# Lightweight convolution and SiLU feed-forward in float32: silu(h) as the stationary operand of the second product, chunks in groups of eight by product shape

## The chip, the cores and the metric

One core of a Trainium2 chip. The number to be predicted is the device time of one execution in microseconds (us), as a median over runs. Engines are written as in the profile: PE is TensorE's matmul, PEld its weight load, DVE is VectorE, ACT is ScalarE, POOL is GpSimd and SP is SyncE, which here issues most of the DMAs.

## The reference

The input x is 8 sequences of 4096 tokens with 192 channels. A causal convolution of 7 taps per head (8 heads of 24 channels, softmax over a head's taps) is followed by a feed-forward block with 2048 hidden units:

```
w = softmax(weight, axis=-1)                      # (8 heads, 7 taps)
x1[b, s, c] = sum_k w[head(c), k] * x_pad[b, s + k, c]
h = x1.reshape(32768, 192) @ w_in                 # w_in (192, 2048)
g = h * (1 / (1 + exp(-h)))                       # silu
out = g @ w_out                                   # w_out (2048, 192)
```

The two matrices arrive as float64 and are rounded to float32 on the chip. All products run in float32.

## The kernel before

The 32768 tokens are worked off in 64 blocks of 512. `load` (L70 to L73) brings a block's rows into `nat`, tokens on partitions. `turn_in` (L180 to L192) turns it on the PE with eight 128x128 transposes into two PSUM tiles `pt`, which ACT copies to `xt`. `conv` (L194 to L204) applies the taps on the DVE, 14 instructions, and leaves `cv`: the first half holds channels 0 to 127 ("a"), the second the other 64 channels ("b") twice, once in each half of the partitions.

The 2048 hidden units are 16 chunks of 128, taken as 8 pairs q. `up` (L207 to L217) makes h of a pair: two products with 128 rows of weights (L210, shape 128\*128 in the profile), then two with 64 rows (L212, 64\*128), which stand in different rows of the PE and run side by side; then ACT writes g = silu(h). `down` (L219 to L237) adds the pair into the block's sums, channels on partitions: the weights w_out are stationary and g moves, 512 columns at a time, into 128 channels (L226, 128\*128) and into 64 (L230, 128\*64), the latter for the two chunks side by side in different columns of the PE. After the eighth pair the sums go to `ot` (L235 on ACT, L236 on DVE). `turn_out` (L239 to L249) turns them back on the PE, four transposes (L246) and four products with `ident2` (L247) that also add the two side-by-side sums, and the DVE copies them to `osb`, which goes out by DMA.

The loop (L254 to L273) sets the order by hand: `up` of pair q, then `down` of pair q - 1. In block b, `turn_in` of block b + 1 comes with q = 1, its `conv` with q = 1 and 2, and `turn_out` of block b - 1 with q = 2. In block 0, `round_w(q)` (L112 to L143, 12 DVE instructions per pair) rounds the weights of a pair ahead of its `up`. A framework places instructions on each engine and adds the waits; each engine runs its own in order.

In the profile a float32 product is two passes, each with a weight load of its own: the 1024 products of L210 show as 2048 MATMULs and 2048 LDWEIGHTS. "Pass" below is one such MATMUL. A transpose is one pass.

Of the kernel before, what the change touches and what calls it, by code (L numbers as in the profile page):

```python
# [9 lines left out]
F32 = mybir.dt.float32  # L10
I32 = mybir.dt.int32
AF = mybir.ActivationFunctionType
ALU = mybir.AluOpType
# [4 lines left out]
def kernel(  # L18
# [5 lines left out]
    moe_w_out: bass.AP,  # L24
    out: bass.AP,
):
    """Everything runs in float32, with channels on partitions between the two turns.

    The two matrices come as float64, which the engines don't have: as raw bits, rounded to
    float32 here (to nearest even; below float32's normal range to 0).  # L30
    A block is TB tokens. Its rows are turned on the PE, the taps are applied along the free axis
    on the DVE, and h = w_in.T @ xT, g = silu(h), oT = w_out.T @ g follow; oT is turned back.
    The D = 192 channels are P = 128 ("a") and R = 64 ("b"). The b rows are held twice, in
    both halves of the partitions, so that the K = 64 products of two chunks of h run side by
    side in the rows of the PE; the M = 64 products of two chunks of g run side by side in its
    columns, and the product that turns their two sums back also adds them.
    """
    nc = tc.nc
    PSUM = bass.MemoryType.PSUM

    B, S, D = x.shape
    H, K = weight.shape
    NT = B * S
    DFF = moe_w_in.shape[1]
    P = 128
    R = D - P
    grp = D // H
# [3 lines left out]
    NB = NT // TB  # L51
    NCH = DFF // P
    NQ = NCH // 2
    assert R == 64 and D == H * grp and S % TB == 0 and DFF == 2 * P * NQ and NQ >= 3

    x_v = x.flatten_outer_dims().rearrange("(n s p) d -> n p s d", s=SUBS, p=P)
# [2 lines left out]
    const = ctx.enter_context(tc.tile_pool(name="const", bufs=1))  # L59
    wpool = ctx.enter_context(tc.tile_pool(name="wp", bufs=3))  # L60
    xpool = ctx.enter_context(tc.tile_pool(name="xp", bufs=3))
    gpool = ctx.enter_context(tc.tile_pool(name="gp", bufs=3))
    opool = ctx.enter_context(tc.tile_pool(name="op", bufs=2))
    ps_h = ctx.enter_context(tc.tile_pool(name="ps_h", bufs=2, space=PSUM))
    ps_o = ctx.enter_context(tc.tile_pool(name="ps_o", bufs=1, space=PSUM))
    ps_t = ctx.enter_context(tc.tile_pool(name="ps_t", bufs=2, space=PSUM))

    nats, xts, cvs, gs, accs, ots = ({} for _ in range(6))

    def load(b):  # L70
        nat = nats[b] = xpool.tile([P, SUBS, P + 2 * R], F32, tag="nat", name="nat")
# [2 lines left out]

    load(0)

    # Each partition's logits: channel c has those of head c // grp.
    wraw = const.tile([P, 2, K], F32, name="wraw")
    for half, p0, c0, c1 in ((0, 0, 0, P), (1, 0, P, D), (1, R, P, D)):
        c = c0  # L80
# [7 lines left out]
            )  # L88
            c = e

    # For a pair of chunks: 2P columns of w_in's a rows, P of its b rows (the first chunk's on
    # partitions 0 to R, the second's above), and D of w_out for each chunk.
    WA, WB, WO = 2 * P, 3 * P, 3 * P + 2 * D
    in32 = moe_w_in.bitcast(I32)
    out32 = moe_w_out.bitcast(I32).rearrange("(q e p) d -> q p e d", e=2, p=P)
# [16 lines left out]
    def round_w(q):  # L112
        words = raws.pop(q).rearrange("p (n t) -> p n t", t=2)
        lo, hi = words[:, :, 0], words[:, :, 1]
        sc, ex, mh, ml, st = (
            wpool.tile([P, WO], I32, tag=f"w_{n}", name=f"w_{n}", bufs=1)
            for n in ("sc", "ex", "mh", "ml", "st")
        )
        m = wpool.tile([P, WO], F32, tag="w_m", name="w_m", bufs=1)

        def two(out, in_, s1, op0, s2, op1):
            nc.vector.tensor_scalar(out, in_, scalar1=s1, scalar2=s2, op0=op0, op1=op1)  # L122

        # sc: the sign and the exponent, as the bits of a float32.
        two(ex, hi, 20, ALU.logical_shift_right, 0x7FF, ALU.bitwise_and)
        two(ex, ex, 896, ALU.max, 896 + 255, ALU.min)
        two(ex, ex, 896, ALU.subtract, float(1 << 23), ALU.mult)
        two(sc, hi, 31, ALU.logical_shift_right, 31, ALU.logical_shift_left)
        nc.vector.tensor_tensor(sc, sc, ex, op=ALU.bitwise_or)
        # The mantissa's upper 21 bits, its next 23, and whether any of the last 9 is set: the  # L130
        # sum of the three rounds once, as the whole would.
        two(mh, hi, 0xFFFFF, ALU.bitwise_and, 0x100000, ALU.bitwise_or)
        nc.vector.tensor_single_scalar(ml, lo, 9, op=ALU.logical_shift_right)
        nc.vector.tensor_single_scalar(st, lo, 0x1FF, op=ALU.bitwise_and)
        nc.vector.tensor_single_scalar(st, st, 1, op=ALU.min)
        nc.vector.scalar_tensor_tensor(  # L136
            out=m, in0=ml, scalar=2.0, in1=st, op0=ALU.mult, op1=ALU.add
        )
        nc.vector.scalar_tensor_tensor(
            out=m, in0=mh, scalar=float(1 << 24), in1=m, op0=ALU.mult, op1=ALU.add  # L140
        )
        nc.vector.scalar_tensor_tensor(  # L142
            out=ws[q], in0=m, scalar=2.0**-44, in1=sc.bitcast(F32), op0=ALU.mult, op1=ALU.mult  # L143
        )

    def w_in_a(q, e):
        return ws[q][:, ts(e, P)]

    def w_in_b(q, e):
        return ws[q][R * e : R * e + R, WA:WB]  # L150

    def w_out_a(q, e):
        return ws[q][:, WB + D * e : WB + D * e + P]

    def w_out_b(q, e):
        return ws[q][:, WB + D * e + P : WB + D * e + D]

    for q in range(NQ):
        load_w(q)
# [1 line left out]

    ident = const.tile([P, P], F32, name="ident")
    make_identity(nc, ident)
    # ident2[p, r] is 1 where p % R == r.
    ident2 = const.tile([P, R], F32, name="ident2")
    nc.vector.tensor_tensor(ident2, ident[:, 0:R], ident[:, R:P], op=ALU.add)

    wmax = const.tile([P, 2], F32, name="wmax")
    wexp = const.tile([P, 2, K], F32, name="wexp")
    wsum = const.tile([P, 2], F32, name="wsum")  # L170
# [9 lines left out]
    def turn_in(b):  # L180
# [5 lines left out]
            nc.gpsimd.tensor_copy(xt[:, :, 0:pad], xts[b - 1][:, :, TB : TB + pad])  # L186
        xts.pop(b - 1, None)
        for half in range(2):
            pt = ps_t.tile([P, TB], F32, tag="pt", name="pt")
            for s in range(SUBS):  # L190
                nc.tensor.transpose(pt[:, ts(s, P)], nat[:, s, ts(half, P)], ident)  # L191
            nc.scalar.copy(xt[:, half, pad : pad + TB], pt)  # L192
# [11 lines left out]
                    out=dst, in0=src[:, k : k + TB], scalar=tap, in1=dst, op0=ALU.mult, op1=ALU.add  # L204
                )

    def up(b, q):  # L207
        hs = [ps_h.tile([P, TB], F32, tag=f"h{e}", name=f"h{e}") for e in range(2)]
        for e in range(2):
            nc.tensor.matmul(hs[e], w_in_a(q, e), cvs[b][:, 0, :], start=True, stop=False)  # L210
        for e in range(2):
            nc.tensor.matmul(  # L212
                hs[e], w_in_b(q, e), cvs[b][R * e : R * e + R, 1, :], start=False, stop=True
            )
        gs[b, q] = [gpool.tile([P, TB], F32, tag=f"g{e}", name=f"g{e}") for e in range(2)]
        for e in range(2):
            nc.scalar.activation(gs[b, q][e], hs[e], AF.Silu)  # L217

    def down(b, q):  # L219
        if q == 0:  # L220
            accs[b] = [ps_o.tile([P, TB], F32, tag=f"acc{i}", name=f"acc{i}") for i in range(2)]
        g = gs.pop((b, q))
        acc_a, acc_b = accs[b]
        first, last = q == 0, q == NQ - 1
        for e in range(2):
            nc.tensor.matmul(  # L226
                acc_a, w_out_a(q, e), g[e], start=first and e == 0, stop=last and e == 1
            )
        for e in range(2):
            nc.tensor.matmul(  # L230
                acc_b[R * e : R * e + R, :], w_out_b(q, e), g[e], start=first, stop=last
            )
        if last:
            ots[b] = [opool.tile([P, TB], F32, tag=f"ot{i}", name=f"ot{i}") for i in range(2)]
            nc.scalar.copy(ots[b][0], acc_a)  # L235
            nc.vector.tensor_copy(ots[b][1], acc_b)  # L236
            del accs[b]  # L237

    def turn_out(b):  # L239
        ot_a, ot_b = ots.pop(b)  # L240
        osb = opool.tile([P, SUBS, D], F32, tag="osb", name="osb")
        for n in range(2):
            pt = ps_t.tile([P, 2, D], F32, tag="pt", name="po")
            for i in range(2):
                s = 2 * n + i
                nc.tensor.transpose(pt[:, i, 0:P], ot_a[:, ts(s, P)], ident)  # L246
                nc.tensor.matmul(pt[:, i, P:D], ot_b[:, ts(s, P)], ident2, start=True, stop=True)  # L247
            nc.vector.tensor_copy(osb[:, 2 * n : 2 * n + 2, :], pt)  # L248
        nc.sync.dma_start(out=out_v[b], in_=osb)  # L249

    turn_in(0)
    for half in range(2):
        conv(0, half)
    for b in range(NB):  # L254
        for q in range(NQ):
            if b == 0:
                round_w(q)
            up(b, q)
            if q:
                down(b, q - 1)  # L260
            elif b:
                down(b - 1, NQ - 1)
            if q == 0 and b + 2 < NB:
                load(b + 2)
            if q == 2 and b:
                turn_out(b - 1)
            if q == 1 and b + 1 < NB:
                turn_in(b + 1)
            if q in (1, 2) and b + 1 < NB:
                conv(b + 1, q - 1)  # L270
        cvs.pop(b)
    down(NB - 1, NQ - 1)
    turn_out(NB - 1)  # L273


# [28 lines left out]
```

## Time and profile before

| | |
|---|---|
| runs (3) | 3199.52, 3199.52 and 3200.01 us, median 3199.52 |
| profiled execution, span from first to last instruction | 3196.9 us |
| lying outside the span, median less span | 2.6 us |
| PE busy | 3152.2 us (99%), 9472 passes |
| PEld busy | 1077.7 us (34%), 9472 loads |
| DVE, ACT, POOL busy | 23%, 21%, 2% |
| mean granted TensorE clock | 0.997 of full speed |

Of the profiled execution only the span is given, not a device time of its own. A PE record runs from a pass's start to a modelled end, and the records of successive passes overlap; so a pass's price is read from the distance between the starts of successive passes, not from its record's length. The chain of waits gives shares of the span by engine and line along the work that ended last.

### The profile page before, as it was taken

Reading aid. Unit: us, or ns where it says so; the run is one execution under the profiler, and the core shown is the slowest. Engines: PE = TensorE matmul, PEld = TensorE weight load, DVE = VectorE, ACT = ScalarE, POOL = GpSimd, SP = SyncE. Lnnn points to the kernel's source line nnn. Section 1 sums busy time; section 2 is a strip of 40 time slices with the busy share of each in tenths; the row PEclk is TensorE's granted clock in tenths of the full one; section 3 lists DMA queues with packets and bytes.
Section 4 is the critical chain, followed back from the end, with each engine's and each line's share of the span. In section 5 each row is a group of like instructions: output and inputs, shape, how many; then the busy total and the mean of one; then the engine's idle time right before and its main releaser. Section 6 shows DMA issues by size and latency. Waiting matters only on the chain.

```text
span 3196.9 us, 23128 instructions
## 1 busy us (share of the span) xinstructions
PE 3152.2 (99%) x9472; PEld 1077.7 (34%) x9472; DVE 735.4 (23%) x1191; ACT 664.9 (21%) x1219; POOL 49.2 (2%) x102
## 2 busy tenths in 40 slices
PE   5999999999999999999999999999999999999999
PEld 1333333333333333333333333333333333333333
DVE  8312122122121221221212212212122122121220
ACT  1212222222122222221221222212212222122121
POOL 3000000000000000000000000000000000000000
PEclk8999999999999999999999999999999999999999
DMA  4000000000000000000000000000000000000000
GB/s 119 12 17 23 12 24 23 12 23 18 17 23 12 23 24 12 23 18 17 23 12 23 23 12 23 19 17 24 12 23 23 12 23 18 17 23 13 16 10 10
DMA packets 103933, 66.50 MB, mean 21 GB/s; under 512 B 36756, under 2 KB 102420, under 8 KB 103828
## 3 DMA queue, kind: packets, MB, share of 16 engines
q1 hardware_dynamic: 101376, 58.73, 6.2%
q0 software_dynamic: 2048, 6.29, 0.7%
q8 instruction: 74, 1.21, 0.2%
q14 instruction: 31, 0.25, 0.0%
q10 hardware_dynamic: 404, 0.01, 0.0%
HBM read 39.85 MB, written 25.17 MB: 20 GB/s over the span
## 4 chain that ended last, share of the span: by engine, by line
PE 98%; DVE 1%; DMA 1%; issue 0%; ACT 0%; POOL 0%; DVEq 0%
PE acc L226 30%; PE h L210 30%; PE h L212 17%; PE acc L230 16%; PE pt L191 2%; PE po L247 1%; PE po L246 1%; DVE cv L203 0%; DMA wraw<-in_weight_dram 0%; DVE w_ex L122 0%; DMA nat<-in_x_dram 0%; DMA raw<-in_moe_w_out_dram 0%; DVE w L142 0%; DVE w_m L136 0%; ACT g L217 0%
## 5 line engine op out<-in xcount | busy, mean ns | idle before, releaser
L217 ACT ACTIVATE g<-h 128x512 f32<-128x512 f32 x1024 | 555.6, 594 | 2304.6 <-PE h L212 2304.6
L210 PE MATMUL h<-cv,w 128*128 128x512 f32 x2048 | 1009.4, 615 | 16.0 <-DVE cv L203 11.9
L226 PE MATMUL acc<-g,w 128*128 128x512 f32 x2048 | 1015.7, 618 | 3.0 <-ACT g L217 3.0
L212 PE MATMUL h<-cv,w 64*128 64x512 f32 x2048 | 578.5, 641 | 0.0
L226 PEld LDWEIGHTS acc<-g,w 128*128 128x128 f32 x2048 | 346.8, 189 | 636.7 <-issue 629.3
L230 PE MATMUL acc<-g,w 128*64 128x512 f32 x2048 | 552.3, 618 | 0.0
L210 PEld LDWEIGHTS h<-cv,w 128*128 128x128 f32 x2048 | 348.2, 190 | 576.0 <-issue 555.6
L203 DVE SCALAR_TENSOR_TENSOR cv<-xt,taps,cv 128x512 f32<-128x512 f32 x768 | 530.1, 744 | 2.2
L236 DVE COPY ot<-acc 128x512 f32<-128x512 f32 x64 | 44.3, 692 | 2020.3 <-PE acc L230 2020.3
L212 PEld LDWEIGHTS h<-cv,w 64*128 64x128 f32 x2048 | 154.3, 185 | 389.8 <-issue 388.3
L230 PEld LDWEIGHTS acc<-g,w 128*64 128x64 f32 x2048 | 101.2, 134 | 388.3 <-issue 388.3
L201 DVE TENSOR_SCALAR cv<-xt,taps 128x512 f32<-128x512 f32 x128 | 57.9, 487 | 401.8 <-ACT xt L192 397.6
L192 ACT COPY xt<-pt 128x512 f32<-128x512 f32 x128 | 69.0, 589 | 153.1 <-issue 130.4
L191 PE MATMUL pt<-ident,nat 128*128 128x128 f32 x512 | 71.5, 284 | 21.0 <-POOL ident masks.py:199 20.8
L191 PEld LDWEIGHTS pt<-ident,nat 128*128 128x128 f32 x512 | 56.1, 144 | 71.3 <-issue 49.5
L247 PEld LDWEIGHTS po<-ident,ot 128*128 128x128 f32 x512 | 77.7, 201 | 0.7 <-DVE ot L236 0.7
L247 PE MATMUL po<-ident,ot 128*128 128x64 f32 x512 | 76.3, 249 | 0.4 <-DVE ot L236 0.4
L248 DVE COPY osb<-po 128x384 f32<-128x384 f32 x128 | 70.2, 549 | 21.4 <-PE po L247 21.3
L246 PE MATMUL po<-ident,ot 128*128 128x128 f32 x256 | 74.5, 291 | 0.0
L186 POOL COPY xt<-xt 128x12 f32<-128x12 f32 x56 | 24.9, 446 | 2977.5 <-DVE cv L201 2234.6
L246 PEld LDWEIGHTS po<-ident,ot 128*128 128x128 f32 x256 | 46.6, 182 | 51.9 <-issue 51.1
L235 ACT COPY ot<-acc 128x512 f32<-128x512 f32 x64 | 37.5, 586 | 52.0 <-PE acc L226 52.0
(31 smaller groups left out, 94.8 us busy)
## 6 DMA issues: line engine op xcount, KB each, us to landing
nat<-in_x_dram SPq DMA_DIRECT2D x64, 384.0 KB, 3.4
out_dram<-osb SPq DMA_DIRECT2D x64, 384.0 KB, 2.6
nat<-in_x_dram SPq DMA_DIRECT2D x64, 128.0 KB, 3.5
raw<-in_moe_w_out_dram POOLq DMA_DIRECT2D x8, 384.0 KB, 5.1
raw<-in_moe_w_in_dram POOLq DMA_DIRECT2D x8, 256.0 KB, 4.6
raw<-in_moe_w_in_dram POOLq DMA_DIRECT2D x16, 64.0 KB, 4.4
wraw<-in_weight_dram ACTq DMA_DIRECT2D x9, 0.7 KB
wraw<-in_weight_dram ACTq DMA_DIRECT2D x2, 0.4 KB, 5.5
```

What stands on the lines that cost most here:

```text
L191: nc.tensor.transpose(pt[:, ts(s, P)], nat[:, s, ts(half, P)], ident)
L192: nc.scalar.copy(xt[:, half, pad : pad + TB], pt)
L201: nc.vector.tensor_scalar(dst, src[:, 0:TB], scalar1=tap, scalar2=None, op0=ALU.mult)
L203: nc.vector.scalar_tensor_tensor(out=dst, in0=src[:, k : k + TB], scalar=tap, in1=dst, op0=ALU.mult, op1=ALU.add)
L210: nc.tensor.matmul(hs[e], w_in_a(q, e), cvs[b][:, 0, :], start=True, stop=False)
L212: nc.tensor.matmul(hs[e], w_in_b(q, e), cvs[b][R * e : R * e + R, 1, :], start=False, stop=True)
L217: nc.scalar.activation(gs[b, q][e], hs[e], AF.Silu)
L226: nc.tensor.matmul(acc_a, w_out_a(q, e), g[e], start=first and e == 0, stop=last and e == 1)
L230: nc.tensor.matmul(acc_b[R * e : R * e + R, :], w_out_b(q, e), g[e], start=first, stop=last)
L246: nc.tensor.transpose(pt[:, i, 0:P], ot_a[:, ts(s, P)], ident)
L247: nc.tensor.matmul(pt[:, i, P:D], ot_b[:, ts(s, P)], ident2, start=True, stop=True)
L248: nc.vector.tensor_copy(osb[:, 2 * n : 2 * n + 2, :], pt)
```

## The change

The second product changes sides. `down(b, c)` now takes one chunk c: for each of the block's four groups of 128 tokens, a 128x128 slice of g is stationary and w_out's 192 columns of that chunk move (one product, L232 of the new kernel). Its result has tokens on partitions, so `turn_out`, `ident2` and the `ot` tiles are gone; `store` copies the two sums to `osb` by two DVE copies and sends them out.

The order of the products is set by half-blocks of eight chunks (GA = 4): four times the 128-row product of h, then eight times the 64-row one (four pairs; the last four of them start their sums with it), then the 128-row product of the last four chunks, and then the second product of all eight chunks. PSUM is divided anew: six tiles `h`, which `pt` shares, and two for the sums. g has 12 buffers.

```diff
-    gpool = ctx.enter_context(tc.tile_pool(name="gp", bufs=3))
+    gpool = ctx.enter_context(tc.tile_pool(name="gp", bufs=3 * GA))
-    ps_h = ctx.enter_context(tc.tile_pool(name="ps_h", bufs=2, space=PSUM))
+    ps_h = ctx.enter_context(tc.tile_pool(name="ps_h", bufs=6, space=PSUM))
     ps_o = ctx.enter_context(tc.tile_pool(name="ps_o", bufs=1, space=PSUM))
-    ps_t = ctx.enter_context(tc.tile_pool(name="ps_t", bufs=2, space=PSUM))
...
-            pt = ps_t.tile([P, TB], F32, tag="pt", name="pt")
+            pt = ps_h.tile([P, TB], F32, tag="h", name="pt")
...
+    def down(b, c):
+        if c == 0:
+            accs[b] = [ps_o.tile([P, 2, D], F32, tag=f"acc{i}", name=f"acc{i}") for i in range(2)]
+        g = gs.pop((b, c))
+        for s in range(SUBS):
+            nc.tensor.matmul(
+                accs[b][s // 2][:, s % 2, :],
+                g[:, ts(s, P)],
+                w_out(c),
+                start=c == 0 and s % 2 == 0,
+                stop=c == NCH - 1,
+                skip_group_check=True,
+            )
+    def store(b):
+        osb = opool.tile([P, SUBS, D], F32, tag="osb", name="osb")
+        for i, acc in enumerate(accs.pop(b)):
+            nc.vector.tensor_copy(osb[:, 2 * i : 2 * i + 2, :], acc)
+        nc.sync.dma_start(out=out_v[b], in_=osb)
...
+        for c0 in range(0, NCH, 2 * GA):
+            c1, c2 = c0 + GA, c0 + 2 * GA
             if b == 0:
+                for q in range(c0 // 2, c2 // 2):
+                    round_w(q)
+            if c0 == 0 and b + 2 < NB:
                 load(b + 2)
+            for c in range(c0, c1):
+                up_a(b, c, True)
+            for q in range(c0 // 2, c1 // 2):
+                up_b(b, q, False)
+                for e in range(2):
+                    act(b, 2 * q + e)
+            for q in range(c1 // 2, c2 // 2):
+                up_b(b, q, True)
+            for c in range(c1, c2):
+                up_a(b, c, False)
+                act(b, c)
+            if c0 == 0 and b + 1 < NB:
                 turn_in(b + 1)
+                for half in range(2):
+                    conv(b + 1, half)
+            for c in range(c0, c2):
+                down(b, c)
         cvs.pop(b)
+        store(b)
```

`up_a` is one 128-row product of h (L205 of the new kernel), `up_b` a pair of 64-row products (L213), `act` one silu.

How the instructions move, first place: PE in the middle of a block of the kernel before, one step of the loop (w_99 and w_100 are the weights of pairs 4 and 5).

```order
L210 MATMUL h_601<-cv,w_100 128x512
L210 MATMUL h_602<-cv,w_100 128x512
L212 MATMUL h_601<-cv,w_100 128x512
L212 MATMUL h_602<-cv,w_100 128x512
L226 MATMUL acc_510<-g_593,w_99 128x512
L226 MATMUL acc_510<-g_594,w_99 128x512
L230 MATMUL acc_511<-g_593,w_99 64x512
L230 MATMUL acc_511<-g_594,w_99 64x512
```

And PE in the changed kernel, from the second half-block of block 1 (w_96 to w_99 are its four pairs' weights there; acc_586 and acc_587 hold two groups of 128 tokens each).

```order
L205 MATMUL h<-cv,w_96 128x512 x2
L205 MATMUL h<-cv,w_97 128x512 x2
L213 MATMUL h<-cv,w_96 128x512 x2
L213 MATMUL h<-cv,w_97 128x512 x2
L213 MATMUL h<-cv,w_98 128x512 x2
L213 MATMUL h<-cv,w_99 128x512 x2
L205 MATMUL h<-cv,w_98 128x512 x2
L205 MATMUL h<-cv,w_99 128x512 x2
L232 MATMUL acc_586<-w_96,g 128x192 x2
L232 MATMUL acc_587<-w_96,g 128x192 x2
L232 MATMUL acc_586<-w_96,g 128x192 x2
```

Before, the shape of the product changes with every line of the pair, four times in two chunks. Now it changes from L205 to L213 and back to L205, in eight chunks; L232 follows with 32 products of the same 128\*128 shape.

Second place: PE where a block's sums are finished. Before, the sums of block 0 are turned back in the third pair of block 1.

```order
L230 MATMUL acc_511<-g_507,w_96 64x512
L246 MATMUL po<-ident,ot_493 128x128
L247 MATMUL po<-ident_151,ot_494 128x64
L246 MATMUL po<-ident,ot_493 128x128
L247 MATMUL po<-ident_151,ot_494 128x64
L246 MATMUL po<-ident,ot_493 128x128
L247 MATMUL po<-ident_151,ot_494 128x64
L246 MATMUL po<-ident,ot_493 128x128
L247 MATMUL po<-ident_151,ot_494 128x64
L210 MATMUL h_573<-cv,w_98 128x512
```

In the changed kernel PE goes from the last second product of block 1 to block 2.

```order
L232 MATMUL acc_586<-w_99,g 128x192 x2
L232 MATMUL acc_587<-w_99,g 128x192 x2
L205 MATMUL h<-cv,w_92 128x512 x2
L205 MATMUL h<-cv,w_93 128x512 x2
```

The eight products of L246 and L247 have left the queue, and nothing stands in their place.

Third place: the waits of PE in the middle of the first half-block of the changed kernel (block 1; `Activation` is ACT's semaphore).

```order
L213 MATMUL h_537<-cv_317,w2_94 128x512
L213 MATMUL h_539<-cv_317,w2_94 128x512
L213 MATMUL h_541<-cv_317,w3_95 128x512 [waits Activation_49]
L213 MATMUL h_543<-cv_317,w3_95 128x512 [waits Activation_49]
L205 MATMUL h_537<-cv_317,w2_94 128x512
```

The fourth pair (h_541, h_543) takes the PSUM tiles of the half-block's first two chunks, and so waits for the silu of these.

## Rows read from the trace of the kernel before

**Rows 1.** The page: busy time, and the clock in 40 slices.

```profile
PE 3152.2 (99%) x9472; PEld 1077.7 (34%) x9472; DVE 735.4 (23%) x1191; ACT 664.9 (21%) x1219; POOL 49.2 (2%) x102
...
PEclk8999999999999999999999999999999999999999
```

**Rows 2.** The page: the chain that ended last, by engine and by line.

```profile
PE 98%; DVE 1%; DMA 1%; issue 0%; ACT 0%; POOL 0%; DVEq 0%
PE acc L226 30%; PE h L210 30%; PE h L212 17%; PE acc L230 16%; PE pt L191 2%; PE po L247 1%; PE po L246 1%; DVE cv L203 0%; DMA wraw<-in_weight_dram 0%; DVE w_ex L122 0%; DMA nat<-in_x_dram 0%; DMA raw<-in_moe_w_out_dram 0%; DVE w L142 0%; DVE w_m L136 0%; ACT g L217 0%
```

**Rows 3.** Timeline of PE: start us, length us, engine, line, operation; one plain pair.

```profile
1005.31 1.98 PE L226 MATMUL acc<-g,w 128*128 128x512 f32 x4
1007.22 1.08 PE L230 MATMUL acc<-g,w 128*64 128x512 f32 x4
1008.23 1.98 PE L210 MATMUL h<-cv,w 128*128 128x512 f32 x4
1010.15 1.13 PE L212 MATMUL h<-cv,w 64*128 64x512 f32 x4
1011.21 1.98 PE L226 MATMUL acc<-g,w 128*128 128x512 f32 x4
```

**Rows 4.** Timeline of PEld: weight loads within that pair's L226 group.

```profile
1005.31 0.30 PEld L226 LDWEIGHTS acc<-g,w 128*128 128x128 f32 x2 [0.76 <-issue]
1005.84 0.19 PEld L226 LDWEIGHTS acc<-g,w 128*128 128x128 f32 x1 [0.24 <-issue]
1006.27 0.19 PEld L226 LDWEIGHTS acc<-g,w 128*128 128x128 f32 x1 [0.24 <-issue]
```

**Rows 5.** Timeline, narrow window: the group's last pass and the next shape's first.

```profile
1006.70 0.59 PE L226 MATMUL acc<-g,w 128*128 128x512 f32 x1
1007.22 0.14 PEld L230 LDWEIGHTS acc<-g,w 128*64 128x64 f32 x2 [0.76 <-issue]
1007.22 0.65 PE L230 MATMUL acc<-g,w 128*64 128x512 f32 x2
```

**Rows 6.** Timeline of PE, narrow windows: the first and the last of eight transposes, and L210.

```profile
1037.72 0.33 PE L191 MATMUL pt<-ident,nat 128*128 128x128 f32 x1
...
1038.54 0.27 PE L191 MATMUL pt<-ident,nat 128*128 128x128 f32 x1
1038.64 0.59 PE L210 MATMUL h<-cv,w 128*128 128x512 f32 x1
```

**Rows 7.** Timeline of PE: turning the last block out, first and last products.

```profile
1044.44 0.33 PE L246 MATMUL po<-ident,ot 128*128 128x128 f32 x1
...
1045.18 0.33 PE L247 MATMUL po<-ident,ot 128*128 128x64 f32 x2
1045.35 0.28 PE L246 MATMUL po<-ident,ot 128*128 128x128 f32 x1
...
1045.63 0.65 PE L210 MATMUL h<-cv,w 128*128 128x512 f32 x1
```

**Rows 8.** Timeline of DVE: the copy at a block's end, blocks 1 and 62.

```profile
147.30 0.69 DVE L236 COPY ot<-acc 128x512 f32<-128x512 f32 x1 [34.69 <-PE acc L230]
...
3145.24 0.69 DVE L236 COPY ot<-acc 128x512 f32<-128x512 f32 x1 [32.03 <-PE acc L230]
```

**Rows 9.** Timeline: a pair's last 64-row passes and its silus on ACT.

```profile
1004.78 0.60 PE L212 MATMUL h<-cv,w 64*128 64x512 f32 x2
...
1005.47 1.08 ACT L217 ACTIVATE g<-h 128x512 f32<-128x512 f32 x2 [4.81 <-PE h L212]
```

**Rows 10.** Groups by line: copies out of PSUM and the convolution.

```profile
L203 DVE SCALAR_TENSOR_TENSOR cv<-xt,taps,cv 128x512 f32<-128x512 f32 x768 | 530.1, 744 | 2.2
...
L192 ACT COPY xt<-pt 128x512 f32<-128x512 f32 x128 | 69.0, 589 | 153.1 <-issue 130.4
...
L248 DVE COPY osb<-po 128x384 f32<-128x384 f32 x128 | 70.2, 549 | 21.4 <-PE po L247 21.3
```

**Rows 11.** Timeline: the end of block 0's rounding on DVE, and the program's last DMA issue.

```profile
88.03 0.96 DVE L142 SCALAR_TENSOR_TENSOR w<-w_m,w_sc 128x768 f32<-128x768 f32 x1
...
3193.19 0.37 SPq L249 DMA_DIRECT2D out_dram<-osb  x1
```

More of the change, by code (lines that the diff above doesn't have):

```diff
@@ L53 @@
     NQ = NCH // 2
+    GA = 4
+    assert NCH % (2 * GA) == 0 and GA % 2 == 0
     assert R == 64 and D == H * grp and S % TB == 0 and DFF == 2 * P * NQ and NQ >= 3
@@ L61 @@
     xpool = ctx.enter_context(tc.tile_pool(name="xp", bufs=3))
-    gpool = ctx.enter_context(tc.tile_pool(name="gp", bufs=3))
+    gpool = ctx.enter_context(tc.tile_pool(name="gp", bufs=3 * GA))
     opool = ctx.enter_context(tc.tile_pool(name="op", bufs=2))
-    ps_h = ctx.enter_context(tc.tile_pool(name="ps_h", bufs=2, space=PSUM))
+    ps_h = ctx.enter_context(tc.tile_pool(name="ps_h", bufs=6, space=PSUM))
     ps_o = ctx.enter_context(tc.tile_pool(name="ps_o", bufs=1, space=PSUM))
-    ps_t = ctx.enter_context(tc.tile_pool(name="ps_t", bufs=2, space=PSUM))
-    nats, xts, cvs, gs, accs, ots = ({} for _ in range(6))
+    nats, xts, cvs, hs, gs, accs = ({} for _ in range(6))
     def load(b):
@@ L150, in w_in_b, with w_out @@
         return ws[q][R * e : R * e + R, WA:WB]
[L152 to L156, printed above, removed]
+    def w_out(c):
+        return ws[c // 2][:, WB + D * (c % 2) : WB + D * (c % 2) + D]
     for q in range(NQ):
@@ L163 @@
     make_identity(nc, ident)
-    ident2 = const.tile([P, R], F32, name="ident2")
-    nc.vector.tensor_tensor(ident2, ident[:, 0:R], ident[:, R:P], op=ALU.add)
     wmax = const.tile([P, 2], F32, name="wmax")
@@ L205, in conv, with up_a, up_b @@
                 )
-    def up(b, q):
-        hs = [ps_h.tile([P, TB], F32, tag=f"h{e}", name=f"h{e}") for e in range(2)]
+    def up_a(b, c, first):
+        if first:
+            hs[b, c] = ps_h.tile([P, TB], F32, tag="h", name="h")
+        nc.tensor.matmul(
+            hs[b, c], w_in_a(c // 2, c % 2), cvs[b][:, 0, :], start=first, stop=not first
+        )
+    def up_b(b, q, first):
         for e in range(2):
-            nc.tensor.matmul(hs[e], w_in_a(q, e), cvs[b][:, 0, :], start=True, stop=False)
-        for e in range(2):
+            if first:
+                hs[b, 2 * q + e] = ps_h.tile([P, TB], F32, tag="h", name="h")
@@ L212, in up @@
             nc.tensor.matmul(
-                hs[e], w_in_b(q, e), cvs[b][R * e : R * e + R, 1, :], start=False, stop=True
-            )
[L215 to L225, printed above, removed]
-            nc.tensor.matmul(
-                acc_a, w_out_a(q, e), g[e], start=first and e == 0, stop=last and e == 1
-            )
[L229 to L237, printed above, removed]
@@ L239, in turn_out @@
-    def turn_out(b):
-        ot_a, ot_b = ots.pop(b)
-        osb = opool.tile([P, SUBS, D], F32, tag="osb", name="osb")
[L242 to L248, printed above, removed]
+                hs[b, 2 * q + e],
@@ new lines, in up_b, with act @@
+                w_in_b(q, e),
+                cvs[b][R * e : R * e + R, 1, :],
+                start=first,
+                stop=not first,
+            )
+    def act(b, c):
+        gs[b, c] = gpool.tile([P, TB], F32, tag="g", name="g")
+        nc.scalar.activation(gs[b, c], hs.pop((b, c)), AF.Silu)
+    def down(b, c):
[3 more added lines that the diff above has]
+        for s in range(SUBS):
+            nc.tensor.matmul(
+                accs[b][s // 2][:, s % 2, :],
[4 more added lines that the diff above has]
+                skip_group_check=True,
+            )
@@ L254 @@
     for b in range(NB):
-        for q in range(NQ):
+        for c0 in range(0, NCH, 2 * GA):
+            c1, c2 = c0 + GA, c0 + 2 * GA
             if b == 0:
[L257 to L263, printed above, removed]
-                load(b + 2)
-            if q == 2 and b:
-                turn_out(b - 1)
-            if q == 1 and b + 1 < NB:
+                for q in range(c0 // 2, c2 // 2):
+                    round_w(q)
+            if c0 == 0 and b + 2 < NB:
+                load(b + 2)
+            for c in range(c0, c1):
[10 more added lines that the diff above has]
+            if c0 == 0 and b + 1 < NB:
                 turn_in(b + 1)
-            if q in (1, 2) and b + 1 < NB:
-                conv(b + 1, q - 1)
+                for half in range(2):
+                    conv(b + 1, half)
+            for c in range(c0, c2):
+                down(b, c)
         cvs.pop(b)
-    down(NB - 1, NQ - 1)
-    turn_out(NB - 1)
+        store(b)
 _INS = ['x', 'weight', 'moe_w_in', 'moe_w_out']
```

## The prediction

> **What bounds the kernel now.** First the page: PE is busy 99% of the span, no other engine over 34%, and the clock is at full speed in nearly all slices [rows 1]. The chain of waits agrees: PE has 98% of it, and by line it is the four products that hold it, L226, L210, L212 and L230 [rows 2]. So only PE time counts, and the question is what each pass costs. Busy time does not tell, since a pass's record overlaps the next; I go to the timeline and read distances between starts.
>
> One plain pair: four passes of L226 take 1.91 us from their start to the next group's, L230 1.01, L210 1.92, L212 1.06, 5.90 in all [rows 3]. Within the L226 group the weight loads of the third and fourth pass start 0.43 apart, and the last pass starts 0.43 after that [rows 4, 5]. A pass of 512 columns thus costs 0.43. Four cost 1.72, two side-by-side rounds (L212, L230) 0.86, and each group has 0.15 to 0.20 more. Where it lies: the last pass starts at 1006.70 and the next group at 1007.22, 0.52 instead of 0.43, so 0.09 is lost in leaving [rows 5]; the first pass of a group starts at 1005.31 and the second at 1005.84 (the third load starts with it), 0.53, so 0.10 is lost in entering: the group's first load begins only as the group does [rows 3, 4]. Inside a group nothing is lost, although L210 changes its weights and its PSUM tile there. The loss belongs to the change of shape. A pair has four: 0.19 + 0.15 + 0.20 + 0.20 = 0.74 us, 12% of it.
>
> The block's other PE work: eight transposes in, at 0.11 a pass, L210 following at the same distance [rows 6], and the turn out, 1045.63 - 1044.44 = 1.19 [rows 7]. Test: 8 x 5.90 + 0.92 + 1.19 = 49.31, less some 0.15 for the entries into L210 that these two stages spare. From block 1 to block 62 the block-end copies are (3145.24 - 147.30) / 61 = 49.15 apart [rows 8]. The prices hold.
>
> **The change, part by part, per block.**
>
> *Passes of h.* Unchanged in number: 32 passes of the 128-row product and 16 side-by-side rounds of the 64-row one, 48 x 0.43 = 20.64.
>
> *Second product.* Before 32 + 16 rounds at 0.43 = 20.64. After: 16 chunks x 4 slices x 2 passes = 128 passes of 192 columns. No row shows this width. Below it stands the transpose's 128 columns at 0.11, above it 512 at 0.43; a straight line gives 0.163 and plain proportion to 512 gives 0.161. I take 0.1625: 20.80. The bounds are 0.11 and 0.43; only loads that do not hide would take it off the line (rivals). So the arithmetic of the swap is nil, +0.16.
>
> *Weight loads.* 128 loads of a full 128x128 instead of 48 loads of stationary operands. A load takes its place in 0.11 (two of 0.19 span 0.30, so the second starts 0.11 after the first [rows 4]), and the next pass's load starts with the pass before it [rows 4, 5]. 0.11 fits under 0.1625. A row where the cover was thin: at the transposes into L210 a full load goes under a 128-column pass and the distance stays 0.10 [rows 6]. A row where it was gone: the two 64-column passes of L247 should take 0.43 / 8 = 0.054 each but take 0.17 together [rows 7]. So a load shows as soon as the pass is shorter than about 0.11, and the cover here is 0.05 per pass. Cost taken: 0.
>
> *Changes of shape.* 32 before at 0.15 to 0.20 (8 x 0.74 = 5.92). After, each half-block goes 128-row, 64-row, 128-row, and all else (transposes, second product, next half-block) is 128\*128: 4 per block x 0.195 = 0.78. Saved 5.14.
>
> *Turn out.* Gone: 1.19 from PE, less the 0.05 or so it spared: saved 1.14. *Turn in:* 8 x 0.11 = 0.88, now without a change of shape around it.
>
> New block: 20.64 + 20.80 + 0.78 + 0.88 = **43.10 us**, 6.05 less than 49.15.
>
> *What hides the rest.* DVE loses the `ot` copy and keeps two copies of 0.55; with the convolution (12 x 0.74 and two shorter) that is some 11 of 43 us [rows 10]. Its convolution of the next block starts about 12 us into the block (24 rounds, 8 transposes, a copy) and has 20 to spare. ACT has 16 silus at 0.49 (two span 1.08, one is 0.59) and two copies of 0.59, 9 us in all [rows 9, 10]. The sums' two PSUM tiles are copied out under the 10 us of h that open the next block; without that cover the price would be some 1.2 per block. SP issues the store behind those copies and the next block's load behind the store; that load is needed a block later. POOL's work stays.
>
> *The wait that is added.* The fourth pair of each half-block takes the PSUM tiles of its first two chunks. Behind it on PE stands everything. From a pair's last passes (1004.78) to its silus' start is 0.69 and to the end of the second one 1.77 [rows 9]. In the new order the fourth pair starts five rounds, 2.15 us, after the first pair's last, and its loads at 1.7 to 2.0. The cover is 0.1 to 0.3 us; if it is gone, the price is that overrun twice a block. Cost taken: 0. g's 12 buffers are released by second products that PE has run before the half-block begins.
>
> *Ends.* Block 0 is bound by the rounding on DVE, whose last instruction ends at 88.99 [rows 11]; the DVE order keeps the same work ahead of it. Behind it come the last pair's h (0.86 + 1.72 + 0.4) and 16 passes (2.6): block 0 done at 94.6. After the last pass come a semaphore and one copy (0.65) and, from the issue of the store, 3196.9 - 3193.19 = 3.7 [rows 11]: 4.4. The last block turns nothing in: -0.9.
>
> Sum: 94.6 + 63 x 43.10 - 0.9 + 4.4 = 2813.4 as the span, against 3196.9. Outside it lay 2.6 (median of the runs shown 3199.52, less the profiled span): **2816 us**, 384 below. A measurement of this kernel tells about 0.2%, 6 us, from no change.
>
> **The rivals.**
>
> *Loads exposed (the slower one).* Every pass of the second product carries a fresh full load, and if loads cannot run beside passes in the same rows of the array each pass costs 0.1625 + 0.11. For it: L247's two passes, where loads do show [rows 7], and the first load of each group, which waits. Price: 128 x 0.11 = 14.1 per block, 57.2; 94.6 + 1.8 + 63 x 57.2 + 3.5 + 2.6 = 3706 us. It decides from 0.1625 + 6.05 / 128 = 0.21 per pass. Against: inside L226 a full load runs under a full pass with no time lost [rows 4, 5]. The Trainium skill, "TensorE: Matmul & The Clock Gate", Part 3, "The mechanism", says that a weight load overlaps a running matmul only where the row groups differ; by it this case would come. The trace disagrees, for loads into the same 128 rows cost nothing inside L226 and L210. Chance 0.03.
>
> *Loads hidden, but one at a time at their record's 0.19.* Then a pass costs 0.19, +3.5 per block: 94.6 + 63 x 46.6 + 3.5 + 2.6, about 3037 us. Against: two loads start 0.11 apart [rows 4]. Chance 0.05.
>
> *The run of eight 64-row products does not chain.* If each pair boundary costs a change of shape, six more per block at 0.2: +1.2, 2891 us. For it: no row shows two such pairs in succession. Against: two chunks of L210 chain without loss. Chance 0.07.
>
> *The tile wait shows.* If the silus come late by 1 us in each half-block, +2.0: 2942 us. For it: the thin cover. Against: ACT is idle before each pair of silus [rows 9]. Chance 0.05.
>
> *The loss is not of shape* but of each wait of PE on another engine, and the change keeps it: the new half-block waits for ACT about eight times; 12 more per block at 0.19 give 2.3 and 2960 us. Against: L212 starts behind L210 in the same chunk, waits for nothing new, and pays. Chance 0.02.
>
> **How the numbers follow.** The forecast case has 0.78. Its own spread: entries and exits half as dear (-25), block 0 earlier or later by 5, or 7 ns more per pass (+56): 2786 to 2872. The range takes in the unchained pairs, to 2900, and leaves out some 0.15. Only the exposed loads make it slower: 0.03; half-exposed loads that end within 0.2% of before: 0.01, out of the 0.05 of the second rival; faster 0.96.
>
> **What would show it.** Second-product passes 0.16 apart; no distance over 0.44 inside runs of one shape; four changes of shape per block at 0.19; blocks 43.1 apart; PE idle nowhere after block 0. Wrong if the passes stand over 0.17 apart, if the fourth pair of 64-row products waits for a silu, or if the clock leaves full speed.

## The result and the profile after

| | before | after |
|---|---|---|
| median of the runs | 3199.69 us (4 runs) | 2813.39 us (4 runs, 2813.10 to 2813.81) |
| ratio, 95% interval | | 0.8793 [0.8781, 0.8806] |
| profiled span | 3196.9 us | 2811.4 us |
| passes on PE, and as many loads | 9472 | 12800 |

The forecast was 2816 us. Measured are 2813.39, 386 us less than before and 2.6 us below the forecast. The first lines of the page, and the chain that ended last by engine and line:

```profile
PE 2764.4 (98%) x12800; PEld 1962.6 (70%) x12800; DVE 697.0 (25%) x1126; ACT 634.9 (23%) x1155; POOL 50.5 (2%) x102
...
PEclk9999999999999999999999999999999999999999
...
PE 97%; DVE 2%; DMA 1%; issue 0%; DVEq 0%
PE acc L232 47%; PE h L205 32%; PE h L213 16%; PE pt L186 2%; DVE cv L198 1%; DMA wraw<-in_weight_dram 0%; DVE w_ex L124 0%; DVE w L144 0%; DVE w_m L141 0%; DVE w_m L138 0%; DVE w_st L137 0%; DMA nat<-in_x_dram 0%; DVE w_st L136 0%; DVE w_sc L124 0%; DVE w_sc L131 0%
```

Against [rows 1, 2]: PE is still the bound, with a third more passes. PEld's share has doubled to 70%, and no load stands in the chain. The timeline of PE after, from the 64-row run of one half-block to the next block, answers to [rows 3, 6, 7]:

```profile
1002.16 3.70 PE L213 MATMUL h<-cv,w 64*128 64x512 f32 x16
1005.79 3.70 PE L205 MATMUL h<-cv,w 128*128 128x512 f32 x8
1009.33 1.04 PE L186 MATMUL pt<-ident,nat 128*128 128x128 f32 x8
1010.20 10.57 PE L232 MATMUL acc<-w,g 128*128 128x192 f32 x64
1020.61 3.60 PE L205 MATMUL h<-cv,w 128*128 128x512 f32 x8
1024.13 3.70 PE L213 MATMUL h<-cv,w 64*128 64x512 f32 x16
1027.77 3.70 PE L205 MATMUL h<-cv,w 128*128 128x512 f32 x8
1031.31 10.56 PE L232 MATMUL acc<-w,g 128*128 128x192 f32 x64
1041.70 3.60 PE L205 MATMUL h<-cv,w 128*128 128x512 f32 x8
```

The prices are read from the starts. L232: 1020.61 - 1010.20 = 10.41 for 64 passes, 0.1627 each. L213: 3.63 for eight rounds, 3.44 and 0.19. L205 behind L213: 3.54, so 0.10 for entering; L205 ahead of L213: 3.52, so 0.08 for leaving. From L205 to L186, L186 to L232 and L232 to L205, all 128\*128, nothing is lost.

The ends of blocks 1 and 62 on DVE, as in [rows 8], and what [rows 11] showed of the two ends of the program:

```profile
87.46 0.96 DVE L144 SCALAR_TENSOR_TENSOR w<-w_m,w_sc 128x768 f32<-128x768 f32 x1
...
94.11 3.60 PE L205 MATMUL h<-cv,w 128*128 128x512 f32 x8
...
136.74 1.21 DVE L244 COPY osb<-acc 128x384 f32<-128x384 f32 x2 [21.63 <-PE acc L232]
...
2764.21 1.21 DVE L244 COPY osb<-acc 128x384 f32<-128x384 f32 x2 [21.62 <-PE acc L232]
...
2806.40 1.21 DVE L244 COPY osb<-acc 128x384 f32<-128x384 f32 x2 [40.99 <-PE acc L232]
2807.64 0.37 SPq L245 DMA_DIRECT2D out_dram<-osb  x1
```

(2764.21 - 136.74) / 61 = 43.07 us per block, forecast 43.10. Block 0 was through at 94.11, forecast 94.6.

### The profile page after: what moved, and what is told of

Same layout as the page of the kernel before. It is cut to its first block, busy times and chain, and to the rows that moved or that the text cites. A ratio compares the mean times of both kernels' runs of the same rounds, so it can differ in the third digit from the quotient of the medians.

```text
span 2811.4 us, 29774 instructions
## 1 busy us (share of the span) xinstructions
PE 2764.4 (98%) x12800; PEld 1962.6 (70%) x12800; DVE 697.0 (25%) x1126; ACT 634.9 (23%) x1155; POOL 50.5 (2%) x102
## 4 chain that ended last, share of the span: by engine, by line
PE 97%; DVE 2%; DMA 1%; issue 0%; DVEq 0%
PE acc L232 47%; PE h L205 32%; PE h L213 16%; PE pt L186 2%; DVE cv L198 1%; DMA wraw<-in_weight_dram 0%; DVE w_ex L124 0%; DVE w L144 0%; DVE w_m L141 0%; DVE w_m L138 0%; DVE w_st L137 0%; DMA nat<-in_x_dram 0%; DVE w_st L136 0%; DVE w_sc L124 0%; DVE w_sc L131 0%
## 5 line engine op out<-in xcount | busy, mean ns | idle before, releaser
L232 PEld LDWEIGHTS acc<-w,g 128*128 128x128 f32 x8192 | 1333.2, 190 | 36.1 <-issue 31.1
L232 PE MATMUL acc<-w,g 128*128 128x192 f32 x8192 | 1353.4, 326 | 1.4 <-ACT g L223 1.4
L223 ACT ACTIVATE g<-h 128x512 f32<-128x512 f32 x1024 | 570.0, 600 | 2142.1 <-PE h L213 1827.1
L205 PE MATMUL h<-cv,w 128*128 128x512 f32 x2048 | 937.5, 600 | 17.6 <-DVE cv L198 14.5
L205 PEld LDWEIGHTS h<-cv,w 128*128 128x128 f32 x2048 | 375.4, 190 | 484.0 <-issue 465.5
L198 DVE SCALAR_TENSOR_TENSOR cv<-xt,taps,cv 128x512 f32<-128x512 f32 x768 | 514.5, 745 | 0.0
L213 PE MATMUL h<-cv,w 64*128 64x512 f32 x2048 | 476.3, 603 | 3.3 <-DVE w L144 3.3
L244 DVE COPY osb<-acc 128x384 f32<-128x384 f32 x128 | 71.4, 558 | 1392.9 <-PE acc L232 1387.0
L213 PEld LDWEIGHTS h<-cv,w 64*128 64x128 f32 x2048 | 198.8, 186 | 270.3 <-issue 247.0
L196 DVE TENSOR_SCALAR cv<-xt,taps 128x512 f32<-128x512 f32 x128 | 58.0, 487 | 705.9 <-ACT xt L187 705.9
L186 PEld LDWEIGHTS pt<-ident,nat 128*128 128x128 f32 x512 | 60.6, 142 | 53.6 <-issue 33.0
L186 PE MATMUL pt<-ident,nat 128*128 128x128 f32 x512 | 67.3, 275 | 20.4 <-POOL ident masks.py:199 20.4
L105 POOL DMA_DIRECT2D raw<-in_moe_w_in_dram x16 | 10.0, 629 | 0.8 <-DMA raw<-in_moe_w_in_dram 0.8
L102 POOL DMA_DIRECT2D raw<-in_moe_w_in_dram x8 | 6.2, 772 | 29.6 <-DVE w_st L136 22.5
```

What stands on the lines that cost most here:

```text
L105: nc.gpsimd.dma_start(out=raw[R * e : R * e + R, 2 * WA : 2 * WB], in_=in32[P:D, c : c + 2 * P])
L196: nc.vector.tensor_scalar(dst, src[:, 0:TB], scalar1=tap, scalar2=None, op0=ALU.mult)
L198: nc.vector.scalar_tensor_tensor(out=dst, in0=src[:, k : k + TB], scalar=tap, in1=dst, op0=ALU.mult, op1=ALU.add)
L205: nc.tensor.matmul(hs[b, c], w_in_a(c // 2, c % 2), cvs[b][:, 0, :], start=first, stop=not first)
L213: nc.tensor.matmul(hs[b, 2 * q + e], w_in_b(q, e), cvs[b][R * e : R * e + R, 1, :], start=first, stop=not first,)
L223: nc.scalar.activation(gs[b, c], hs.pop((b, c)), AF.Silu)
```

## The experiments

The theory to test: what a pass costs is its columns; what is lost beside is 0.2 us per change of shape; a load is free as long as the pass before it is longer than the load's place. Three rivals stood against it: the gain comes from the swap of sides itself, the loss is one of waits, loads do not overlap.

### The swap alone (e1) and the grouping alone (e2)

e1 leaves the kernel before pair by pair, and takes the new second product and its store.

```diff
     def down(b, q):
...
+        for e in range(2):
+            for s in range(SUBS):
+                nc.tensor.matmul(
+                    accs[b][s // 2][:, s % 2, :],
+                    g[e][:, ts(s, P)],
+                    w_out(2 * q + e),
...
-            if q == 2 and b:
-                turn_out(b - 1)
```

> The swap of sides alone: silu(h) is stationary and nothing is turned back, but the order stays pair by pair (128-row, 64-row, then the second product of the pair before). Shape theory: two changes of shape per pair at 0.196, 16 per block; block = 48 x 0.43 + 20.8 + 0.88 + 3.1 = 45.4 us, 2.34 more than the change, total about 2960 us. Rival (the loss is one of waits, not of shape): no dearer per block than the change but for a few waits, under 2850. Rival (the swap itself brings the gain): close to the change, within 20 us of 2813.

Measured: 2968.97 us, ratio 0.9281 [0.9265, 0.9296]. (A ratio is to the kernel before on the same chip, with its 95% interval.) The timeline of PE, one pair, and the ends of blocks 5 and 62 on DVE:

```profile
1004.98 1.88 PE L207 MATMUL h<-cv,w 128*128 128x512 f32 x4
1006.79 1.13 PE L209 MATMUL h<-cv,w 64*128 64x512 f32 x4
1007.85 2.87 PE L222 MATMUL acc<-w,g 128*128 128x192 f32 x16
1010.55 1.88 PE L207 MATMUL h<-cv,w 128*128 128x512 f32 x4
...
328.17 1.21 DVE L233 COPY osb<-acc 128x384 f32<-128x384 f32 x2 [29.21 <-PE acc L222]
...
2919.53 1.21 DVE L233 COPY osb<-acc 128x384 f32<-128x384 f32 x2 [29.22 <-PE acc L222]
```

A pair takes 5.57 instead of 5.90, and (2919.53 - 328.17) / 57 = 45.46 us per block, as the shape theory has it (45.4). The block ends before these lie 43.4 to 44.6 apart, chiefly because the transposes of blocks 1 to 5 stand in block 0 on PE's timeline. The total is 9 us above the expectation, mainly because block 0 ended later; its rounding, 6 us late, is in the last section.

e2 takes the order of the change and keeps the second product of before, first the 128-column products of the eight chunks, then their 64-column ones, and the turn out beside the turn in.

```diff
...
+        for c in range(c0, c2):
+            nc.tensor.matmul(acc_a, w_out_a(c), gs[b, c], start=c == 0, stop=c == NCH - 1)
+        for c in range(c0, c2):
+            e = c % 2
+            nc.tensor.matmul(
+                acc_b[R * e : R * e + R, :], w_out_b(c), gs.pop((b, c)), start=c < 2, stop=c >= NCH - 2
+            )
...
+            if c0 == 0 and b:
+                turn_out(b - 1)
+            down(b, c0, c2)
```

> The grouping alone: eight chunks by shape, but the second product as before (w_out stationary, 128 and then 64 columns, sums turned back). Shape theory: per half-block four changes, two at 0.196 (into and out of the 64-row product), one at about 0.14 into the 64-column one and one at 0.19 out of it, 1.45 per block, and the turn out at 1.15 without a change around it; block = 20.6 + 20.6 + 1.45 + 0.87 + 1.15 = 44.7 us, total about 2920 us. If the swap brought the gain: near 3150.

Measured: 2924.88 us, ratio 0.9142 [0.9128, 0.9155]. Timeline of PE, a half-block from the last 128-row run on:

```profile
1021.85 3.70 PE L212 MATMUL h<-cv,w 128*128 128x512 f32 x8
1025.38 7.03 PE L237 MATMUL acc<-g,w 128*128 128x512 f32 x16
1032.34 3.65 PE L240 MATMUL acc<-g,w 128*64 128x512 f32 x16
1035.93 3.70 PE L212 MATMUL h<-cv,w 128*128 128x512 f32 x8
```

L240 runs 3.59 for eight rounds, 0.15 over 3.44, the same excess that a single L230 pair had [rows 3]: the loss goes with the run, not with its length. The block ends on DVE lie 44.76 apart (140.84 to 2871.20 in 61 blocks).

So per block: 49.15 before, 45.46 with the swap alone, 44.76 with the grouping alone, 43.07 with both. Neither is the whole, and their gains of 3.69 and 4.39 add to 2.00 more than the 6.08 of both. That is counted twice: the changes around the 64-column product are removed by the swap, and made rare by the grouping.

### Groups of four (e3)

```diff
-    GA = 4
+    GA = 2
```

> The change with GA = 2: groups of four chunks, 8 changes of shape per block instead of 4, nothing else on PE. Shape theory: 4 x 0.196 = 0.78 more per block, 43.85 us, total 2813 + 49 = 2863 us. Rival (only waits cost): as the change, 2813, or a little more.

Measured: 2864.46 us, ratio 0.8954 [0.8941, 0.8968]. A half of the old half-block, on the timeline of PE:

```profile
1028.05 1.88 PE L205 MATMUL h<-cv,w 128*128 128x512 f32 x4
1029.86 1.99 PE L213 MATMUL h<-cv,w 64*128 64x512 f32 x8
1031.78 1.99 PE L205 MATMUL h<-cv,w 128*128 128x512 f32 x4
1033.60 5.36 PE L232 MATMUL acc<-w,g 128*128 128x192 f32 x32
1038.80 1.88 PE L205 MATMUL h<-cv,w 128*128 128x512 f32 x4
```

Passes, loads and second products are the same in number, only the changes are eight instead of four. (The buffers of g, 3 * GA, become six with the same edit; no pass comes late for it in these rows.) L213's four rounds take 1.92 where eight take 3.63: 0.20 over 1.72, once per run. The block ends are 43.87 apart (138.59 to 2814.61), 0.80 more, 0.20 per change. Of e1 to e3 this is the one that leaves each product as it is and moves only their order, and so it is what shows the price.

### Halves of 96 columns (e4)

The edit, with changes of indentation left out:

```diff
...
+            for i in range(2):
                 nc.tensor.matmul(
-                    accs[b][s // 2][:, s % 2, :],
+                    accs[b][s // 2][:, s % 2, ts(i, D // 2)],
                     g[:, ts(s, P)],
-                    w_out(c),
-                    start=c == 0 and s % 2 == 0,
+                    w_out(c)[:, ts(i, D // 2)],
+                    start=c == 0 and s % 2 == 0 and i == 0,
...
```

> The change with w_out's 192 columns moved in two products of 96, so that each weight load has a pass of 96 columns (about 0.083 us) beside it and there are twice the loads. Theory that a load runs beside the pass before it and shows only by what it is longer: pass distance 0.107 to 0.11, 64 x (4 x 0.108 - 0.325) = 6.8 more per block, total about 3245 us. Rival, loads do not overlap passes in the same rows: 0.083 + 0.107 = 0.19 per pass, 27.8 more per block, total about 4570 us. Rival, loads are hidden whatever the width: 2835 us.

Measured: 3306.94 us, ratio 1.0337 [1.0322, 1.0353], slower than the kernel before. On the timeline of PE one half-block's second product and what follows it:

```profile
1024.24 14.43 PE L233 MATMUL acc<-w,g 128*128 128x96 f32 x128
1038.51 3.63 PE L205 MATMUL h<-cv,w 128*128 128x512 f32 x8
```

14.27 for 128 passes, 0.1115 each. The columns alone need 0.43 x 96 / 512 = 0.081, and the load in a row after them would make 0.19. So the load runs beside the pass before it, and sets the distance itself once the pass is shorter: its place is 0.1115. The theory had 0.108, and that difference, 256 x 0.0035 = 0.9 per block or 56 us, is nearly all of the miss.

### Five and four tiles for h (e5, e6)

```diff
-    ps_h = ctx.enter_context(tc.tile_pool(name="ps_h", bufs=6, space=PSUM))
+    ps_h = ctx.enter_context(tc.tile_pool(name="ps_h", bufs=5, space=PSUM))
```

e6 has `bufs=4`. These test the wait that the change adds, whose cover the prediction put at 0.1 to 0.3 us.

> The change with five PSUM tiles for h instead of six: a chunk of the 64-row run now waits for the silu of the chunk five places back. From the trace of the change a silu is through 1.32 us after its pair's last 64-row pass (the next ones 1.82, 2.31, 2.80), and a load needs 0.11 ahead of its pass. Cover theory (six tiles leave 0.2 us at the fourth pair, nothing is lost there): the second chunk of the fourth pair starts at 2.42 instead of 2.15, 0.27 lost per half-block, 34 us in all, 2848 us. Rival (the wait with six tiles costs already): the loss grows by a whole pair, 0.86 per half-block, 108 us, 2920 us. Rival (the order of PE's loads hides it): 2813.

> The same with four tiles: the third pair waits for the first pair's silus (loads from 1.32 and 1.82, passes from 1.43 and 1.93 instead of 1.29), the fourth for the second's (2.31 and 2.80, passes from 2.42 and 2.91 instead of 2.15). Cover theory: 0.76 lost per half-block, 1.5 per block, 96 us, 2909 us. Rival (hidden): 2813.

Measured: e5 2847.56 us, ratio 0.8899 [0.8884, 0.8914]; e6 2909.10 us, 0.9092 [0.9079, 0.9106]. The 64-row run of a half-block, and what follows it, on e5's timeline of PE and of PEld:

```profile
1013.97 3.97 PE L213 MATMUL h<-cv,w 64*128 64x512 f32 x16
...
1016.32 0.79 PEld L213 LDWEIGHTS h<-cv,w 64*128 64x128 f32 x4 [0.19 <-ACT g L223]
...
1017.87 3.70 PE L205 MATMUL h<-cv,w 128*128 128x512 f32 x8
```

and on e6's of PE:

```profile
1012.45 4.46 PE L213 MATMUL h<-cv,w 64*128 64x512 f32 x16
1016.84 3.70 PE L205 MATMUL h<-cv,w 128*128 128x512 f32 x8
```

With six tiles the run takes 3.63, with five 3.90, with four 4.39: 0.27 and 0.76 more, the two expected delays to the hundredth. e5's load that waits is put down to ACT. In the change itself the last load of the fourth pair's first round comes at 1004.51, 0.1 behind its neighbour's; its pass starts at 1004.84, and a load takes 0.11, so 0.22 is left (1004.84 - 0.11 - 1004.51):

```profile
1004.51 0.18 PEld L213 LDWEIGHTS h<-cv,w 64*128 64x128 f32 x1
```

So the wait is there, and is covered.

### The convolution of block 1 later (e7), beside the change again (e8)

Seeing that block 0 is bound by the rounding, I moved the only other large piece of DVE work out of its way.

```diff
             if c0 == 0 and b + 1 < NB:
                 turn_in(b + 1)
+            if c0 == (2 * GA if b == 0 else 0) and b + 1 < NB:
                 for half in range(2):
                     conv(b + 1, half)
```

> The change with the convolution of block 1 (14 DVE instructions, 9 us) put behind the rounding of all weights in the DVE's order, instead of between the fifth pair's steps. Nothing else is moved. If block 0 ends with the rounding (theory), the last rounding ends some 7 us earlier, at 81, block 0 on PE 5 us earlier, and the total is about 2808 us, 5 less than the change. Rival (PE or the silus bind block 0, or block 1 then waits for its convolution): no difference.

> The change itself on the same chip, to compare with: 2813 us.

Measured: e7 2808.44 us (2807.87 to 2809.62), ratio to before 0.8778 [0.8765, 0.8791]; e8 2813.74 us (2813.40 to 2814.29), 0.8794 [0.8781, 0.8807]. The two intervals against the kernel before overlap, the two ranges of times on the same chip do not: 5.3 us less (0.19%), the fastest version of this study. The end of the rounding on DVE and the first products of block 1 on PE, in e7 and then in e8:

```profile
80.49 0.95 DVE L144 SCALAR_TENSOR_TENSOR w<-w_m,w_sc 128x768 f32<-128x768 f32 x1
...
90.50 1.88 PE L205 MATMUL h<-cv,w 128*128 128x512 f32 x4
...
87.81 0.96 DVE L144 SCALAR_TENSOR_TENSOR w<-w_m,w_sc 128x768 f32<-128x768 f32 x1
...
95.22 3.60 PE L205 MATMUL h<-cv,w 128*128 128x512 f32 x8
```

The rounding ends 7.3 us earlier (81.4 for 88.8) and block 1 begins 4.7 earlier (90.50 for 95.22); the two spans differ by these 4.7 (2807.8 and 2812.5). The rest of the 7.3 is not had, because PE now comes 9.1 us behind the last rounding instead of 6.4: two pairs' second products stand there, in e8 one pair's.

## Why the prediction was right

- *What bounds the kernel.* PE before and after, idle nowhere after block 0; e1 to e6 each moved the block by what they did on PE. Shown.
- *Second product, 0.1625 a pass.* 0.1627 measured, from a width that the trace before did not have. 128 passes are 20.82 for 20.80.
- *Weight loads, cost 0.* Right: 128 full loads a block, and a pass distance that is the columns' own (0.161 in proportion to 512). Before there were 64 loads, not 48 (32 of L226 and 32 of L230). The bound of about 0.11, read from the two loads of [rows 4], is 0.1115 in e4. L247's two short passes do not show it, though the prediction took them so: they take 0.17 together, 0.085 each with a full load each [rows 7], under 0.1115. Why the loads find room there stays open; the bound is shown for the long run of products in e4. So in the change the cover is 0.051 per pass, and thinner than it looks: at 96 columns it is gone and the whole change with it.
- *Changes of shape, 32 to 4, 5.14 saved.* The largest term. The after trace pays 0.08 to leave and 0.10 to enter, e3 gives 0.20 per change by itself, and L213 here and L240 in e2 show that a run of eight rounds pays no more than a run of two.
- *Turn out, 1.14.* Gone. In e2, where it stands among 128\*128 work, the eight products still take 1003.98 - 1002.85 = 1.13 per block.
- *The added wait, cost 0.* Right, with 0.22 us in hand: a load of the fourth pair does wait for a silu, which the prediction had named as a sign of being wrong, but no pass is late for it, and e5 and e6 show what each missing tile would have cost.
- *Ends.* Block 0 at 94.11 for 94.6. From the issue of the last store to the end 3.8 for 3.7. Between span and device time lie 2.0 us for 2.6.
- *The sum.* Of the 2.6 us by which the forecast is too high, 63 x 0.027 = 1.7 are the block's (0.43 is 0.429 in finer steps), 0.5 block 0 and 0.6 what lies outside the span, less 0.2 at the tail.

The rivals: exposed loads fall by L232's 0.1627 and by e4, where 0.19 was their figure and 0.1115 came; loads one at a time at 0.19 fall by the same two. The Trainium skill's rule that a load overlaps a running matmul only where the row groups differ ("TensorE: Matmul & The Clock Gate", Part 3, "The mechanism") is against these runs: all loads of L232 go to the same 128 rows as the pass beside them. The unchained run of eight falls by L213's 3.63. The loss of waits falls by e1 and e3, for which it had under 2850 and about 2813 and which took 2968.97 and 2864.46, and by L232: some of its 64 loads carry a wait for ACT, and their passes stand the columns' own 0.1627 apart. The late silu falls in the change, and comes true in e5 and e6.

## What to carry to other kernels

When one engine is the bound, price a step by the distance between starts and look for what a group has beyond its passes: here 12% of the time lay between products of different shape, and the order of the work, not the work, decided it. Two edits that remove the same loss do not add; try each alone before crediting either. A swap of stationary and moving operand is free only while the moving side is longer than a load's place: at 192 columns it is, at 96 the kernel is slower than it was.

## What was not expected of the hardware

In e1 the rounding ended at 94.4 instead of 88.4. DVE waited for raw weights, whose DMAs POOL issues, and POOL stood in one small copy, which takes 0.46 on average in the change's trace. POOL's timeline, and the DVE instruction that waited:

```profile
55.23 15.75 POOL L183 COPY xt<-xt 128x12 f32<-128x12 f32 x1 [9.32 <-DVE cv L200]
70.92 0.54 POOL L100 DMA_DIRECT2D raw<-in_moe_w_in_dram  x1
...
76.30 0.56 DVE L122 TENSOR_SCALAR w_ex<-raw 128x768 int32<-128x768 int32 x1 [5.38 <-DMA raw<-in_moe_w_out_dram]
```

The copy lasts as long as DVE works on the rounding without a gap, and is over when DVE runs dry at 70.92. e7 has the same copy at 18.63 us, and there it held nothing up, since the last weights' DMAs had been issued ahead of it. In e7 DVE does not run dry; the copy is over at 77.16, just after the first instruction of a convolution (L196) has started between two of the rounding's:

```profile
58.53 18.63 POOL L181 COPY xt<-xt 128x12 f32<-128x12 f32 x1
...
77.03 0.47 DVE L196 TENSOR_SCALAR cv<-xt,taps 128x512 f32<-128x512 f32 x1
```

The change's own trace has the same: its copy at 57.92 is over at 58.67, and an L196 starts at 58.54. The Trainium skill, "SBUF — State Buffer", "SBUF: two separate sides", says that one port pair is held in turn by GpSimd and by DVE, the latter in some modes or with two inputs in SBUF while GpSimd reads there, and that the other is fully blocked for the instruction. The traces agree with that; that the copy stays out between one of the rounding's instructions and the next as well, and comes in at an L196, is what they add. That the port is the cause is argued from these times, and which of the rounding's instructions does it was not tried.

The other surprise is the 0.0035 us by which a load's place in e4, 0.1115, is longer than the 0.108 of the expectation: small, but 56 us in e4.
